# Weights converted with the sign set by ScalarE's parametric ReLU; retention with 64-row score matmuls, q scaled on GpSimd and x split from PSUM

## The chip, the cores and the metric

The kernel runs on one core of one Trainium2 chip. The metric is the device time of one execution in microseconds (us), median of several runs. Engines are named as in the profile: PE is TensorE (its matmuls; PEld its weight loads), DVE is VectorE, ACT is ScalarE, POOL is GpSimd, SP is SyncE, whose queue issues all DMAs here.

## The reference

Four batches of 576 tokens and 8 heads of 64 go through retention (attention with a decay and no softmax), and then through two MLPs of 512 x 2048. All weights arrive as float64.

```
scores = scale * (q @ k.T)
ret    = scores * D          # D[i, j] = gamma_h ** (i - j) for i >= j, else 0
x      = (ret @ v), heads side by side: 2304 tokens x 512
x1     = square(relu(x @ w_in)) @ w_out            # first MLP
h      = x1 @ w_in2
out    = (h * clip(h + 3, 0, 6) / 6) @ w_out2      # second MLP
```

## The kernel before, in words

**Numbers.** A product in about full float32 is made of three fp32r matmuls: weight and input are each split in a rounded part (index 0) and the rest (index 1), and the three larger products are added up in PSUM. So each of the 16 slices of d_ff (f) costs 12 matmuls into `h` (`h_part`, line 296) and 12 (second MLP, 384 tokens: 9) into the accumulators `acc` (`a_part`, lines 340 and 342). Retention's own matmuls are plain fp32; the trace shows each of these as two instructions.

**Weights.** Each slice has two halves (512 columns of w_in, 512 of w_out), and each half is converted from the 64 bits of its float64 numbers. `scale_w`: ACT multiplies the high word as if it were a float32 (line 109) and turns the low word into rounding bits (line 110). `narrow_w`, on DVE: shift the high word left (124), put the sign bit back from the high word (125), and add the low bits as an integer (127, on POOL for the second MLP's w_out halves, else on DVE). `split_w`: a rounded part by ACT (138) or DVE (136), and the rest by a subtraction on POOL (139). The 32 halves of the first MLP are converted during its first block of 512 tokens; the 32 of the second are spread over 27 steps, from the first MLP's last block into the second MLP's first block.

**Retention** goes by chunks of 128 tokens. `prep_chunk` scales v (POOL; chunk 0 on DVE). `scores` multiplies k by q for each of 8 heads: k is kept by the dims of two heads, one head at a time, with noughts in the other head's 64 rows, so that every matmul uses all 128 rows (204); DVE applies the mask from PSUM (210). `values` makes `o` (223, and 233 for the state of earlier chunks), scales it by the query's decay (246 on DVE, or 243 on ACT and 244 on POOL for chunks 0 to 2), and splits x: rounded part on ACT (249), rest on POOL (250). `states` carries the state on (262, 274 to 277).

**Order.** The schedule is manual: every engine takes its instructions in program order and waits by semaphores. First come chunks 0 to 3, then 160 steps of (MLP, block, f). A step issues `h_part` of the next step before `a_part` of its own, with weight conversions and a quarter of the next block's chunk (prep, scores, values, states, one in each of four steps) in between. In the first block the step's DVE work is: `narrow_w` of a w_out half, its rounded part, the split of `g`, and `narrow_w` of a w_in half. In the first block ACT makes all of `r` and of the rounded `g` (306, 308, 316); in the other blocks DVE squares (310) and rounds (318).

## Time and profile before

| | us |
|---|---|
| runs | 928.20, 926.77, 928.01 (median 928.01) |
| span of the profiled execution, first to last instruction | 924.4 |
| PE busy | 891.0 (96%) |
| DVE busy | 499.9 (54%) |
| ACT busy | 240.3 (26%) |
| POOL busy | 205.9 (22%) |

The profiled execution's time is shown as its span alone; the runs lie 2.4 to 3.8 us above it, which is what stands before the first and behind the last instruction. A busy PE is not a PE at its peak, since matmuls are pipelined and their ends are modelled: how fast PE goes is read from start to start. The averages hide three kinds of stage. DVE is busy nearly all the time in two of them, about 32 to 144 us and 480 to 595 us, and lightly used in the rest.

### The profile page before, as it was taken

Reading aid. Unit: us, or ns where it says so; the run is one execution under the profiler, and the core shown is the slowest. Engines: PE = TensorE matmul, PEld = TensorE weight load, DVE = VectorE, ACT = ScalarE, POOL = GpSimd, SP = SyncE. Lnnn points to the kernel's source line nnn. Section 1 sums busy time; section 2 is a strip of 40 time slices with the busy share of each in tenths; the row PEclk is TensorE's granted clock in tenths of the full one; section 3 lists DMA queues with packets and bytes.
Section 4 is the critical chain, followed back from the end, with each engine's and each line's share of the span. In section 5 each row is a group of like instructions: output and inputs, shape, how many; then the busy total and the mean of one; then the engine's idle time right before and its main releaser. Section 6 shows DMA issues by size and latency. Waiting matters only on the chain.

```text
span 924.4 us, 11741 instructions
## 1 busy us (share of the span) xinstructions
PE 891.0 (96%) x4716; PEld 760.1 (82%) x4716; DVE 499.9 (54%) x772; ACT 240.3 (26%) x411; POOL 205.9 (22%) x169
## 2 busy tenths in 40 slices
PE   7899999999999999999999997899999999999998
PEld 6677768999888899998877786788888888888997
DVE  5899995433433334433889899633343334333333
ACT  2666662111111111112444553211111111111111
POOL 5555551110101001120356356300100110010000
PEclk9899999999999999999999999999999999999999
DMA  8934511121201111105565300100020002000100
GB/s 287 364 100 155 206 46 46 46 69 47 80 23 46 46 46 46 46 1 166 202 215 169 126 0 12 59 11 1 12 80 1 12 0 72 1 9 0 46 1 35
DMA packets 26549, 67.73 MB, mean 73 GB/s; under 512 B 3200, under 2 KB 5376, under 8 KB 26496
## 3 DMA queue, kind: packets, MB, share of 16 engines
q1 hardware_dynamic: 26496, 67.00, 21.2%
q8 instruction: 37, 0.61, 0.3%
q14 instruction: 16, 0.13, 0.0%
HBM read 57.55 MB, written 9.44 MB: 72 GB/s over the span
## 4 chain that ended last, share of the span: by engine, by line
PE 72%; DVE 17%; DMA 5%; issue 3%; ACT 2%; POOL 1%; SPq 1%; DVEq 0%; ACTq 0%; POOLq 0%
PE h L296 33%; PE acc L342 18%; PE acc L340 15%; DVE wt L127 4%; DVE wt L125 4%; DVE wt L124 3%; DVE g L319 2%; PE sc L204 2%; DMA raw<-w_dram 2%; DVE g L318 2%; DMA kt<-qk_dram 1%; PE o L223 1%; PE o L233 1%; ACT r L306 1%; DVE r L313 1%
## 5 line engine op out<-in xcount | busy, mean ns | idle before, releaser
L296 PE MATMUL h<-x,w 128*128 128x512 f32 (+2 forms) x1932 | 425.9, 368 | 5.3 <-ACT w L138 3.0
L296 PEld LDWEIGHTS h<-x,w 128*128 128x128 f32 x1932 | 352.3, 188 | 57.7 <-POOL w L139 5.7
L340 PE MATMUL acc<-g,w 128*128 128x512 f32 (+1 forms) x960 | 217.2, 373 | 5.1 <-POOL w L139 1.8
L342 PE MATMUL acc<-w,g 128*128 128x512 f32 x864 | 212.8, 393 | 9.1 <-DVE g L318 8.2
L342 PEld LDWEIGHTS acc<-w,g 128*128 128x128 f32 x864 | 160.8, 188 | 46.1 <-DVE g L318 9.8
L340 PEld LDWEIGHTS acc<-g,w 128*128 128x128 f32 x960 | 172.0, 188 | 31.6 <-POOL w L139 3.9
L313 DVE SCALAR_TENSOR_TENSOR r<-r,h 128x512 f32<-128x512 f32 (+1 forms) x80 | 50.7, 633 | 202.9 <-ACT r L312 202.9
L310 DVE TENSOR_TENSOR r<-r 128x384 f32<-128x384 f32 (+1 forms) x64 | 42.3, 662 | 173.0 <-ACT r L306 172.9
L312 ACT ACTIVATE r<-h,con 128x512 f32<-128x512 f32 (+1 forms) x80 | 51.5, 644 | 283.0 <-PE h L296 274.4
L319 DVE TENSOR_TENSOR g<-r,g 128x512 fp32r<-128x512 f32 (+1 forms) x160 | 120.7, 754 | 6.3 <-ACT g L316 1.3
L139 POOL TENSOR_TENSOR w<-wt,w 128x512 fp32r<-128x512 f32 x64 | 96.4, 1510 | 82.3 <-ACT w L138 48.8
L306 ACT ACTIVATE r<-h 128x512 f32<-128x512 f32 (+1 forms) x80 | 44.1, 551 | 240.5 <-PE h L296 231.4
L318 DVE CAST g<-r 128x512 fp32r<-128x512 f32 (+1 forms) x144 | 71.6, 497 | 14.3
L385 POOL TENSOR_TENSOR x<-x1r,x 128x512 fp32r<-128x512 f32 (+1 forms) x20 | 25.4, 1271 | 240.1 <-DVE x L384 238.4
L250 POOL TENSOR_TENSOR x<-x,x 128x512 fp32r<-128x512 f32 (+1 forms) x19 | 23.6, 1245 | 208.7 <-ACT x L249 208.7
L125 DVE SCALAR_TENSOR_TENSOR wt<-raw,wt 128x512 int32<-128x512 int32 x64 | 58.3, 911 | 2.2
L138 ACT ACTIVATE w<-wt 128x512 fp32r<-128x512 f32 x48 | 30.3, 631 | 87.4 <-DVE wt L127 53.4
L127 DVE CUSTOM_DVE_ANT_0 wt<-raw,wt 128x1024 uint16<-128x1024 uint16 x48 | 46.9, 977 | 3.5
L204 PE MATMUL sc<-q,kt 128*128 128x128 f32 x288 | 38.0, 285 | 5.8 <-POOL kt L392 4.2
L204 PEld LDWEIGHTS sc<-q,kt 128*128 128x128 f32 x288 | 36.4, 199 | 7.4 <-POOL kt L392 4.2
L109 ACT ACTIVATE raw<-raw 128x512 f32<-128x512 f32 x64 | 42.5, 663 | 0.0
L110 ACT ACTIVATE raw<-raw 128x512 int32<-128x512 uint32 x64 | 42.4, 662 | 0.0
(33 smaller groups left out, 325.0 us busy)
## 6 DMA issues: line engine op xcount, KB each, us to landing
raw<-w_dram SPq DMA_DIRECT2D x64, 512.0 KB, 6.0
kv<-kv_dram SPq DMA_DIRECT2D x14, 512.0 KB, 3.2
q<-qk_dram SPq DMA_DIRECT2D x18, 256.0 KB, 2.9
kt<-qk_dram SPq DMA_DIRECT2D x36, 128.0 KB, 3.1
out_dram<-ev SPq DMA_DIRECT2D x18, 256.0 KB, 2.3
x<-ev SPq DMA_DIRECT2D x12, 256.0 KB, 2.1
x1r<-x SPq DMA_DIRECT2D x12, 256.0 KB, 3.5
kv<-kv_dram SPq DMA_DIRECT2D x8, 256.0 KB, 5.4
```

The lines of the kernel that those rows point to most:

```text
L125: nc.vector.scalar_tensor_tensor(ti, high, -(2**31), ti, ALU.bitwise_and, ALU.bitwise_or)
L127: eng.tensor_tensor(ti, ti, low, ALU.add)
L139: nc.gpsimd.tensor_tensor(w[:, 1, :], t, w[:, 0, :].bitcast(F32), ALU.subtract)
L204: nc.tensor.matmul(sc[e][:, p, :], kt[:, e, p, :], q[:, p, :], start=True, stop=True)
L296: nc.tensor.matmul(hp[:, ts], w[:, wi, c * P : (c + 1) * P], x[:, xi, c, ts], start=k == 0, stop=k == 3 * NC - 1,)
L306: nc.scalar.activation(r, hp[:, :nb], AF.Relu)
L312: nc.scalar.activation(r, hp[:, :nb], AF.Relu, bias=con3)
L313: nc.vector.scalar_tensor_tensor(r, r, 6.0, hp[:, :nb], ALU.min, ALU.mult)
L318: nc.vector.tensor_copy(g[:, 0, :nb], r)
L319: nc.vector.tensor_tensor(g[:, 1, :nb], r, g[:, 0, :nb].bitcast(F32), ALU.subtract)
L340: nc.tensor.matmul(acc[d][:, :nb], wt[:, sl], gt, start=first, stop=stop)
L342: nc.tensor.matmul(acc[d], gt[:, sl], wt, start=first, stop=stop)
```

## The change

Weights: ACT's scaling of the high word becomes a parametric ReLU with the slope -(2^32) for negative numbers. A negative number comes out positive, with an exponent that the shift by three turns into a set sign bit, so DVE's instruction for the sign goes. The integer addition is now on DVE for all halves. Retention: q is scaled by its decay ahead of the scores (POOL; chunk 0 on DVE), so `o` needs no factor and x is split directly from PSUM, rounded part on ACT and rest on DVE. k comes without noughts, in one DMA, and a head's scores use the 64 rows of that head alone, the two heads of a pair in turn. The table of q's factors is loaded earlier. First MLP: `r` times `h` from PSUM on DVE replaces the square, in the first block that on ACT.

```diff
-            nc.scalar.activation(high.bitcast(F32), high.bitcast(F32), AF.Copy, scale=2.0**-112)
+            high = high.bitcast(F32)
+            nc.scalar.activation(high, high, AF.Prelu, scale=2.0**-112, alpha=-(2.0**32))
...
-            nc.vector.scalar_tensor_tensor(ti, high, -(2**31), ti, ALU.bitwise_and, ALU.bitwise_or)
-            eng = nc.gpsimd if ph and i else nc.vector
-            eng.tensor_tensor(ti, ti, low, ALU.add)
+            nc.vector.tensor_tensor(ti, ti, low, ALU.add)
...
-        for e in range(2):
-            r = slice(64 * e, 64 * e + 64)
-            nc.sync.dma_start(kt[r, e], qk[c, r, 1, :].rearrange("p (n t) -> p n t", n=NPAIR))
+        if c == 0:
+            nc.sync.dma_start(con[:, QD0:], cst[:, QD0:])
+        nc.sync.dma_start(kt, qk[c, :, 1, :].rearrange("p (n t) -> p n t", n=NPAIR))
...
     def prep_chunk(c, eng):
+        q = ch[c][0]
+        eng.tensor_tensor(q, q, qd3, ALU.mult)
...
-                nc.tensor.matmul(
-                    sc[e][:, p, :], kt[:, e, p, :], q[:, p, :], start=True, stop=True
-                )
+                r = slice(64 * e, 64 * e + 64)
+                nc.tensor.matmul(sc[e][:, p, :], kt[r, p, :], q[r, p, :], start=True, stop=True)
...
-            t = tmpp.tile([P, np_, P], F32, tag="tmp", name=f"x_{c}_{i}")
             hi = xt[:, 0, ps, off : off + P]
-            if c < n0 and parts == 1:
-                nc.scalar.activation(t, o, AF.Copy)
-                nc.gpsimd.tensor_tensor(t, t, qd3[:, ps], ALU.mult)
-            else:
-                nc.vector.tensor_tensor(t, o, qd3[:, ps], ALU.mult)
+            nc.scalar.activation(hi, o, AF.Copy)
             if then is not None:
                 then()
-            nc.scalar.activation(hi, t, AF.Copy)
-            nc.gpsimd.tensor_tensor(xt[:, 1, ps, off : off + P], t, hi.bitcast(F32), ALU.subtract)
+            nc.vector.tensor_tensor(xt[:, 1, ps, off : off + P], o, hi.bitcast(F32), ALU.subtract)
...
             nc.scalar.activation(r, hp[:, :nb], AF.Relu)
-            if blk == 0:
-                nc.scalar.activation(r, r, AF.Square)
-            else:
-                nc.vector.tensor_tensor(r, r, r, ALU.mult)
+            nc.vector.tensor_tensor(r, r, hp[:, :nb], ALU.mult)
...
-    for t in kts:
-        for e in range(2):
-            nc.gpsimd.memset(t[64 * e : 64 * e + 64, 1 - e], 0.0)
```

How instructions move on the engines: first DVE in the first block of the first MLP, in the step that prepares w_out half 2 and, behind it, w_in half 4 (`wt` is a half's float32, `raw` its words, `g` the input of the second product, `p` the masked scores). Before:

```order
L124 TENSOR_SCALAR wt_2_1_480<-raw_2_1_152 128x512
L125 SCALAR_TENSOR_TENSOR wt_2_1_480<-raw_2_1_152,wt_2_1_480 128x512
L127 ISA wt_2_1_480<-raw_2_1_152,wt_2_1_480 128x1024
L136 CAST w_2_1_487<-wt_2_1_480 128x512
L319 TENSOR_TENSOR g_0_2_506<-r_0_2_503,g_0_2_506 128x512
L210 TENSOR_TENSOR p_4_523<-sc_4_513,con 128x512
L210 TENSOR_TENSOR p_4_525<-sc_4_514,con 128x512
L124 TENSOR_SCALAR wt_4_0_527<-raw_4_0_448 128x512
L125 SCALAR_TENSOR_TENSOR wt_4_0_527<-raw_4_0_448,wt_4_0_527 128x512
L127 ISA wt_4_0_527<-raw_4_0_448,wt_4_0_527 128x1024
```

and now:

```order
L126 TENSOR_SCALAR wt_2_1_448<-raw_2_1_136 128x512
L127 ISA wt_2_1_448<-raw_2_1_136,wt_2_1_448 128x1024
L136 CAST w_2_1_454<-wt_2_1_448 128x512
L298 TENSOR_TENSOR r_0_2_470<-r_0_2_470,h_0_2_457 128x512
L307 TENSOR_TENSOR g_0_2_473<-r_0_2_470,g_0_2_473 128x512
L207 TENSOR_TENSOR p_4_490<-sc_4_480,con 128x512
L207 TENSOR_TENSOR p_4_492<-sc_4_481,con 128x512
L126 TENSOR_SCALAR wt_4_0_494<-raw_4_0_416 128x512
L127 ISA wt_4_0_494<-raw_4_0_416,wt_4_0_494 128x1024
```

Two sign instructions are gone, and the multiplication of `r` stands between the cast and the split of `g`; the ACT instruction that rounds `g` stands, in its own queue, between these two.

Second, POOL in the first steps of the first block, where the weights' rests (`w`) and chunk 4's preparation (`kv`, `q`) share the queue. Before:

```order
L139 TENSOR_TENSOR w_2_0_419<-wt_2_0_415,w_2_0_419 128x512
L139 TENSOR_TENSOR w_1_1_426<-wt_1_1_422,w_1_1_426 128x512
L190 TENSOR_TENSOR kv_216<-kv_216,con 128x512
L139 TENSOR_TENSOR w_3_0_484<-wt_3_0_456,w_3_0_484 128x512
L139 TENSOR_TENSOR w_2_1_487<-wt_2_1_480,w_2_1_487 128x512
```

and now:

```order
L139 TENSOR_TENSOR w_2_0_388<-wt_2_0_385,w_2_0_388 128x512
L139 TENSOR_TENSOR w_1_1_394<-wt_1_1_391,w_1_1_394 128x512
L186 TENSOR_TENSOR q_199<-q_199,con 128x512
L188 TENSOR_TENSOR kv_200<-kv_200,con 128x512
L139 TENSOR_TENSOR w_3_0_451<-wt_3_0_425,w_3_0_451 128x512
L139 TENSOR_TENSOR w_2_1_454<-wt_2_1_448,w_2_1_454 128x512
```

The scaling of q comes behind the weights' rests and ahead of v's; a chunk's scores, one step later on PE, now need it.

## Rows read from the trace of the kernel before

**Rows 1.** The page's first line.

```profile
span 924.4 us, 11741 instructions
```

**Rows 2.** Three stretches of the windows view: the first block of the first MLP; its blocks 1 to 3; and the stage of the second MLP's weights. Columns: stretch and its length; busy us and instructions of PE, PEld, DVE, ACT, POOL; granted clock; DMA share; GB/s.

```profile
31.80:143.70 111.90, 105.96 (x554) 81.70 (x553) 106.03 (x141) 72.13 (x125) 58.88 (x43) 1.00 0.43 152
143.70:414.80 271.10, 271.10 (x1730) 247.52 (x1730) 108.03 (x202) 35.62 (x65) 34.60 (x37) 1.00 0.14 46
...
479.50:595.20 115.70, 100.93 (x458) 83.02 (x457) 104.85 (x133) 51.74 (x92) 60.82 (x43) 0.99 0.22 73
```

**Rows 3.** Timeline of PE in block 1 (384 tokens). Columns here and in the other timelines: start us, duration us with the drain of the last one, engine, line, operation, out<-in, shape, count, and in brackets the idle time before it with its releaser.

```profile
152.80 2.24 PE L296 MATMUL h<-x,w 128*128 128x384 f32 x12
154.88 1.95 PE L204 MATMUL sc<-q,kt 128*128 128x128 f32 x16
156.58 2.33 PE L340 MATMUL acc<-g,w 128*128 128x384 f32 x12
158.76 2.24 PE L296 MATMUL h<-x,w 128*128 128x384 f32 x12
160.93 1.09 PE L223 MATMUL o<-p,kv 128*64 128x128 f32 x16
161.96 1.16 PE L233 MATMUL o<-q,state 128*128 128x128 f32 x8
...
167.23 0.69 PE L262 MATMUL st<-kv 128*64 128x64 f32 x16
...
176.28 1.95 PE L204 MATMUL sc<-q,kt 128*128 128x128 f32 x16
```

**Rows 4.** Timeline of PE in the first block (512 tokens): the scores of chunks 5 and 6, four steps apart.

```profile
74.71 1.95 PE L204 MATMUL sc<-q,kt 128*128 128x128 f32 x16
...
104.17 1.95 PE L204 MATMUL sc<-q,kt 128*128 128x128 f32 x16
```

**Rows 5.** Timeline of DVE in the first block.

```profile
112.43 0.42 DVE L124 TENSOR_SCALAR wt<-raw 128x512 int32<-128x512 int32 x1
112.88 0.69 DVE L125 SCALAR_TENSOR_TENSOR wt<-raw,wt 128x512 int32<-128x512 int32 x1
113.61 0.69 DVE L127 CUSTOM_DVE_ANT_0 wt<-raw,wt 128x1024 uint16<-128x1024 uint16 x1
...
115.50 1.57 DVE L127 CUSTOM_DVE_ANT_0 wt<-raw,wt 128x1024 uint16<-128x1024 uint16 x1
...
118.05 0.68 DVE L246 TENSOR_TENSOR x<-o,con 128x512 f32<-128x512 f32 x1
```

**Rows 6.** Timeline of POOL in the first block.

```profile
115.04 1.48 POOL L139 TENSOR_TENSOR w<-wt,w 128x512 fp32r<-128x512 f32 x1 [2.70 <-ACT w L138]
```

**Rows 7.** Timeline of PE in the stage of the second MLP's weights: the start of four groups of h.

```profile
479.54 0.84 PE L296 MATMUL h<-x,w 128*128 128x512 f32 x3
...
521.71 2.27 PE L296 MATMUL h<-x,w 128*128 128x384 f32 x12
...
525.90 2.27 PE L296 MATMUL h<-x,w 128*128 128x384 f32 x12
...
595.20 2.88 PE L296 MATMUL h<-x,w 128*128 128x512 f32 x12
```

**Rows 8.** Timeline of DVE in the same stage.

```profile
522.43 0.36 DVE L318 CAST g<-r 128x384 fp32r<-128x384 f32 x1
...
525.35 0.55 DVE L313 SCALAR_TENSOR_TENSOR r<-r,h 128x384 f32<-128x384 f32 x1
526.00 1.04 DVE L318 CAST g<-r 128x384 fp32r<-128x384 f32 x1
527.07 0.56 DVE L319 TENSOR_TENSOR g<-r,g 128x384 fp32r<-128x384 f32 x1
...
528.00 1.67 DVE L125 SCALAR_TENSOR_TENSOR wt<-raw,wt 128x512 int32<-128x512 int32 x1
...
560.55 0.42 DVE L384 CAST x<-x1r 128x512 fp32r<-128x512 f32 x1
```

**Rows 9.** Timeline of POOL in the same stage.

```profile
525.51 1.31 POOL L127 TENSOR_TENSOR wt<-wt,raw 128x512 int32<-128x512 int32 x1 [1.56 <-DVE wt L125]
```

**Rows 10.** Timeline of DVE in the first 32 us.

```profile
19.57 1.41 DVE L125 SCALAR_TENSOR_TENSOR wt<-raw,wt 128x512 int32<-128x512 int32 x1
21.13 1.54 DVE L127 CUSTOM_DVE_ANT_0 wt<-raw,wt 128x1024 uint16<-128x1024 uint16 x1
...
24.35 1.31 DVE L277 TENSOR_TENSOR state<-state,con 64x256 f32<-64x256 f32 x1
```

**Rows 11.** Timeline of PE there: chunk 3's values.

```profile
26.35 1.12 PE L223 MATMUL o<-p,kv 128*64 128x128 f32 x8 [3.31 <-DVE state L276]
```

**Rows 12.** The groups by line. Columns: line, engine, operation, out<-in, shapes, count | busy us, mean ns | idle us before and its releasers.

```profile
L109 ACT ACTIVATE raw<-raw 128x512 f32<-128x512 f32 x64 | 42.5, 663 | 0.0
...
L316 ACT ACTIVATE g<-r 128x512 fp32r<-128x512 f32 x16 | 10.1, 632 | 0.5
...
L243 ACT ACT_TABLE_LOAD x1 | 1.3, 1283 | 0.7 <-PEq L521 0.7
```

**Rows 13.** The weight loads of the scores (128 columns) and of the values (64 columns), from the view of one line. Columns: duration ns min/median/max, first and last start, forms.

```profile
L204 PEld LDWEIGHTS sc<-q,kt x288: 186/192/338, 4.2 to 406.2; 128*128 128x128 f32 x144
...
L223 PEld LDWEIGHTS o<-p,kv x288: 132/137/232, 12.2 to 411.4; 128*64 128x64 f32 x144
```

More of the change, by code (lines that the diff above doesn't have):

```diff
@@ L147, in retention_moe_kernel @@
     state = [apool.tile([P, NPAIR, P], F32, tag=f"s{i}", name=f"state{i}") for i in range(2)]
-    kts = [apool.tile([P, 2, NPAIR, P], F32, tag=f"kt{i}", name=f"kt{i}") for i in range(2)]
-    kts += [wpool.tile([P, 2, NPAIR, P], F32, tag=f"w{NF - 1}_{i}", name=f"kt{i + 2}") for i in range(2)]
     n0 = BLOCKS[0][0][0] // P
@@ L162, in load_chunk @@
             kv_t = wpool.tile([P, 2, DM], F32, tag=f"w{NF - 3}_{c % 2}", name=f"kv_{c}")
-            q, kt = t[:, 0], kts[c]
         else:
-            q = rawp.tile([P, NPAIR, P], F32, tag="q", name=f"q_{c}")
+            t = rawp.tile([P, 2, NPAIR, P], F32, tag="q", name=f"q_{c}")
             kv_t = rawp.tile([P, 2, DM], F32, tag="kv", name=f"kv_{c}")
-            kt = kts[c % 2]
+        q, kt = t[:, 0], t[:, 1]
         nc.sync.dma_start(q, qk[c, :, 0, :].rearrange("p (n t) -> p n t", n=NPAIR))
-        for e in range(2):
-            r = slice(64 * e, 64 * e + 64)
-            nc.sync.dma_start(kt[r, e], qk[c, r, 1, :].rearrange("p (n t) -> p n t", n=NPAIR))
+        if c == 0:
+            nc.sync.dma_start(con[:, QD0:], cst[:, QD0:])
+        nc.sync.dma_start(kt, qk[c, :, 1, :].rearrange("p (n t) -> p n t", n=NPAIR))
         if c == 0:
@@ L397, in retention_moe_kernel @@
     load_chunk(1)
-    nc.sync.dma_start(con[:, QD0:], cst[:, QD0:])
     load_chunk(2)
```

## The prediction

> **What bounds the kernel now.** I read the windows by stage first. In blocks 1 to 3 PE is busy for all of the 271.1 us and DVE for 108: PE bounds, and only PE work taken away counts. In the first block and in the stage of the second MLP's weights DVE is busy for 106.0 of 111.9 us and 104.9 of 115.7, while PE has gaps [rows 2]. After 595 us nothing changes. So there are four places: the start, the two stages of DVE, and retention on PE in between.
>
> The timelines then give rates. On PE a group of 12 matmuls of 384 columns starts the next one 2.08 us later where 2.24 is printed, so 0.16 is drain [rows 3]; 12 of 512 columns, printed as 2.88, take 2.72 [rows 7]. A step of 512 tokens is thus 5.44 us on PE, and a step of the second MLP's block of 384 takes 525.90 - 521.71 = 4.19 [rows 7].
>
> On DVE the same instruction has two durations. The addition takes 0.69 us, and 1.57 where it begins inside a subtraction of POOL (115.04 to 116.52) [rows 5, 6]; the sign instruction takes 0.69 or 1.67 [rows 5, 8], the cast 0.36 or 1.04 [rows 8]. An instruction on SBUF data that meets one of POOL is held, by 0.9 to 1.0 us. Those that read PSUM (0.68 and 0.55) show no such stretch in these rows [rows 5, 8]. DVE's load is therefore its own work plus POOL's instructions as far as they meet it.
>
> **The change part by part.**
>
> *Start.* Chunk 3's values wait 3.31 us for DVE [rows 11]. Ahead of them on DVE stand a sign instruction (1.41, goes), a held addition (1.54) and a held state update (1.31, by its shape no longer than 0.69) [rows 10]. POOL's scaling and subtraction of x, which hold them, go. I count 1.41 for the sign, 0.85 and 0.6 for the holds, a second 0.6 for the other half's update, less 0.69 for a subtraction of x that DVE gains: 2.8, say 3. Upper bound the whole wait, 3.3. Lower bound -1: chunk 0's scores now need the table and a DVE multiplication of about 0.69 first.
>
> *First block.* Chunks 5 and 6 lie 104.17 - 74.71 = 29.46 us apart, four steps [rows 4]. In these DVE loses 8 sign instructions, 8 x 0.69 = 5.5, and gains 4 multiplications from PSUM, 4 x 0.69 = 2.8 (priced as the 0.68 of such an operand). It also gains a wait: the split of `g` stands right behind the multiplication and needs ACT's rounding in between, 0.63 [rows 12] and two hand-overs, some 0.73 a step or 2.9 in four, and 0.6 once where x's subtraction waits for ACT. Queued behind these waits are the next half's shift and addition. But POOL's subtraction for the w_out half starts behind the cast, so it now runs under the multiplication and the wait (1.4 us together), and its hold goes: 4 x 0.88 = 3.5. The other holds stay; on POOL q's scaling replaces x's subtraction. Sum: 29.46 - 5.5 + 2.8 + 2.9 + 0.6 - 3.5 = 26.7. PE could do it in 4 x 5.44 + 4.64 for retention (block 1's chunks are 176.28 - 154.88 = 21.40 apart, less four steps of 4.19 [rows 3, 7]) less 0.6 = 25.8, so PE is close behind as the next bound. The stage's 111.9 us are 3.8 such cycles [rows 2]; I count 3.6, since the first h at its start is not paced by DVE. Gain 3.6 x 2.76 = 9.9. Bounds: 13 if DVE falls to PE's 25.8, and 0 if the holds stay and the waits come on top (30.2, rounded to no gain).
>
> *Scores.* 16 instructions take 156.58 - 154.88 = 1.70 us, 106 ns each. The nearest row in which neighbours use different halves of the array is that of the values: 161.96 - 160.93 = 1.03 [rows 3]. There the halves are of columns, here of rows. I take 1.03 and add 0.09 for the change of shape: 2.17 us from h to o against 2.08 from h to scores [rows 3]. 1.70 - 1.12 = 0.58 a chunk, in the 11 chunks of blocks 1 to 3: 6.4. Upper bound two full halves, 0.85 and so 0.76 a chunk, 8.4; lower bound below nothing, see the first rival. Block 0's three chunks are inside its term.
>
> *Second MLP's weights.* From 479.54 to 595.20 PE does 10 groups of 512 columns and 16 steps of 4.19: 27.2 + 67.0 = 94.2 of 115.7 us, so 21.4 are lost [rows 7]. 32 halves in 27 steps are 1.19 a step. DVE's step before: 0.55 + 0.36 + 0.56 for `r` and `g` [rows 8], 1.19 x (0.42 + 0.69) for shift and sign, 0.59 x 0.69 for the additions that it has, 3.2 in all; and 1.78 POOL instructions (1.19 subtractions, 0.59 additions of 1.31 [rows 9]) at a hold of 0.98, 1.7: 4.9 against PE's 4.19. Now shift and addition, 1.19 x 1.11, and 1.19 holds: 1.47 + 1.32 + 1.17 = 3.96, under 4.19. What stays late are the four steps that also cast a piece of x1 (0.42 [rows 8]) and meet its POOL subtraction (0.98): 5.4 against 4.19, 1.2 x 4 = 5. Gain 21.4 - 5 = 16.4. Upper bound 21.4; lower bound what DVE loses by itself, 32 x 0.69 - 16 x 0.69 = 11.
>
> *At nothing.* The parametric ReLU instead of a copy: 0.66 [rows 12], and even twice that would be 32 x 0.66 = 21 us more in a block where ACT idles for 40 of 112 [rows 2]; that idle time is its cover. q's 14 later scalings on POOL, at about 1.3 each: POOL idles for more than 230 of the 271 us of blocks 1 to 3 [rows 2], and a whole step lies between preparation and scores. Fewer DMA issues and the earlier table: in the term of the start. The squares of the other blocks: DVE idles there.
>
> **Sum.** 3 + 9.9 + 6.4 + 16.4 = 35.7 off the span of 924.4 [rows 1]: 888.7. The runs' median stands 3.6 above that span, so 892.3; I say 892.
>
> **The rivals.**
>
> 1. *Weight loads pace the scores* (15%). A load of 128 columns is printed 55 ns longer than one of 64 (192 against 137) [rows 13], 0.86 ns a column, so 110 for 128 columns; if loads went one by one, 16 would take 1.76 us however few rows they have, and with 0.09 the scores would be 0.15 slower than 1.70: -1.7 instead of +6.4, 900. Against it: the state's 16 instructions, each with a load of 64 columns, are printed as 0.69 with their drain [rows 3], under the 16 x 55 = 0.88 of loads one by one. That was between halves of columns; for rows nothing shows it. The Trainium skill has this rival as a rule ("TensorE: Matmul & The Clock Gate", section LDWEIGHTS): a load takes its columns over 1.2 GHz, whatever the rows, an estimated 1.71 us for 16 of 128 columns. Applied one by one it would give the state's 16 loads an estimated 0.85, and the trace does not agree.
>
> 2. *The first block stays bound by DVE* (15%). The new order DVE, ACT, DVE inside each step, with in-order queues on both, costs what the sign instruction gave; the bound above, no gain there: 902. For it: DVE has hardly any idle time there to put the wait in.
>
> 3. *Both stages fall to PE's pace* (8%): 13 and 21.4 instead of 9.9 and 16.4: 884; with the upper bounds of the others, 882.
>
> 4. *Slower: ACT changes tables* (3%). If the parametric ReLU is not held together with copy and ReLU, each of its 64 uses needs two table loads of 1.28 us [rows 12]. In the first block ACT, busy for 72.1 of 111.9 [rows 2], less 16 squares of 0.63 (line 308 is of the kind of line 316), would get 32 x 2.56 = 82 more: 144 against the 102 forecast, 42 more; in the later stage 51.7 + 82 = 134 against 99, 35 more: 892 + 77 = 969. It decides from about three uses in four: ACT's idle time, 40 and 47, covers the first, and 164 x 0.75 - 87 = 36 is the sum above. Against it: the changed program's ACT queue, like the one before, begins with one table load and has no other. The Trainium skill ("ScalarE: Activation LUTs", section Table sets: the hidden batching unit) says that cheap functions such as relu and copy are in every set and only a switch of sets costs; its section on the evaluator also says that the parametric ReLU's slope select is not reachable from a kernel, which would make wrong weights and not another time.
>
> That q on POOL stalls PE at the scores is no case of its own: it would cost chunk 4 once, where the queue is full with the first weights.
>
> **How the numbers follow.** The forecast has 59%, the rivals 15, 15, 8 and 3. The forecast's own range is 885 to 900: its terms' bounds seldom fall to one side together. Rivals 1 and 2 lie at 900 and 902, both together, or with the lower bound of the late stage, at 908; rival 3 at 882. I give 882 to 907, which leaves out rival 4 and the ends of combinations. A measurement of this kernel tells apart about 0.2%, 1.9 us. All cases but the fourth are faster by far more: faster 0.95, same 0.02 for a sum of mishaps, slower 0.03.
>
> **What would show it.** Scores of 16 instructions in about 1.1 us in block 1; chunks 5 and 6 about 26.7 us apart, with a wait of some 0.7 ahead of the split of `g`; in the stage of the second MLP's weights one held DVE instruction a step where there are two, and PE's 115.7 us down to about 99; the rest after it as long as before. I am wrong if scores stay at 1.7, if the chunks stay 29 apart, if DVE's instructions in the late stage are held as often as now, or if ACT shows table loads.

## The result, and the profile after

The changed kernel takes 892.73 us (median of 4 runs, 892.26 to 893.54) against 927.53 for the kernel before in the same session: a ratio of 0.963, with an interval of 0.9617 to 0.9645. The forecast was 892. The profiled execution's span fell from 924.4 to 891.1 us.

I cut both traces at the same five places, read from PE's timeline, and use the table for every run below. *Start*: up to the first `h`. *First block*: to the first `h` of 384 columns. *Blocks 1 to 3*: to the first `h` of 512 columns behind the last state product. *Late*: to the second group of `h` of 512 columns behind the second MLP's first block (595.20 in [rows 7]); it is the stretch of 115.7 us in [rows 2] and the 64.7 us ahead of it, which the change left as they were. *Rest*: to the end.

| us | start | first block | blocks 1 to 3 | late | rest | span |
|---|---|---|---|---|---|---|
| before | 31.82 | 111.92 | 271.06 | 180.40 | 329.20 | 924.4 |
| after | 28.42 | 104.10 | 265.55 | 163.63 | 329.40 | 891.1 |
| gain | 3.40 | 7.82 | 5.51 | 16.77 | -0.20 | 33.3 |
| forecast | 3 | 9.9 | 6.4 | 16.4 | 0 | 35.7 |

The windows of the changed kernel, with the columns of [rows 2]: first block, blocks 1 to 3, the stage of the second MLP's weights, and a piece of the first block.

```profile
28.42:132.52 104.10, 100.60 (x557) 81.02 (x554) 89.21 (x127) 60.93 (x108) 53.15 (x41) 0.98 0.44 162
132.52:398.07 265.55, 265.55 (x1730) 237.87 (x1728) 109.72 (x202) 35.34 (x66) 35.39 (x37) 1.00 0.14 47
462.86:561.70 98.84, 96.24 (x457) 82.60 (x456) 87.62 (x122) 52.72 (x92) 40.96 (x31) 1.00 0.26 85
43.60:48.00 4.40, 4.40 (x15) 3.49 (x14) 3.57 (x5) 2.08 (x5) 2.75 (x3) 0.63 0.00 0
```

Against [rows 2], DVE's load fell from 106.0 to 89.2 us in the first block and from 104.9 to 87.6 in the late stage, and it is idle for longer in both: 104.10 - 89.21 = 14.9 and 98.84 - 87.62 = 11.2 us (in the first block 10.5 of it ahead of the splits of `g`, where DVE waits for ACT). In blocks 1 to 3 PE is busy all the time as before; only its own work became less.

PE's timeline in block 1, to be held against [rows 3]:

```profile
141.57 2.25 PE L287 MATMUL h<-x,w 128*128 128x384 f32 x12
143.74 1.16 PE L203 MATMUL sc<-q 64*128 64x128 f32 x16
144.84 2.35 PE L328 MATMUL acc<-g,w 128*128 128x384 f32 x12
```

From start to start the scores take 1.10 us where they took 1.70; the `h` ahead of them takes 2.17 where it took 2.08, which is the 0.09 for the change of shape.

PE's timeline in the first block, chunks 4, 5 and 6, beside [rows 4]:

```profile
42.48 1.20 PE L203 MATMUL sc<-q 64*128 64x128 f32 x16 [2.03 <-POOL q L186]
43.61 4.54 PE L328 MATMUL acc<-g,w 128*128 128x512 f32 x12
47.99 1.32 PE L287 MATMUL h<-x,w 128*128 128x512 f32 x5
...
70.13 1.16 PE L203 MATMUL sc<-q 64*128 64x128 f32 x16
...
96.90 1.23 PE L203 MATMUL sc<-q 64*128 64x128 f32 x16 [0.24 <-POOL q L186]
```

Chunks 5 and 6 are 26.77 us apart on PE; forecast 26.7, before 29.46. (DVE's own cycle is longer, as shown below.) At chunk 4 PE waits 2.03 us for POOL, and the next 12 matmuls take 47.99 - 43.61 = 4.38 us where such a group takes 2.72 [rows 7]. The last window above shows why: the granted clock is 0.63 there, a mean between the levels of 1.2 and 2.4 GHz.

DVE's timeline in the first block, beside [rows 5], and POOL's beside [rows 6]:

```profile
113.60 1.41 DVE L136 CAST w<-wt 128x512 fp32r<-128x512 f32 x1
114.93 0.68 DVE L298 TENSOR_TENSOR r<-r,h 128x512 f32<-128x512 f32 x1
116.30 0.69 DVE L307 TENSOR_TENSOR g<-r,g 128x512 fp32r<-128x512 f32 x1 [0.70 <-ACT g L304]
```

```profile
113.33 1.39 POOL L139 TENSOR_TENSOR w<-wt,w 128x512 fp32r<-128x512 f32 x1 [3.20 <-ACT w L138]
115.09 1.30 POOL L139 TENSOR_TENSOR w<-wt,w 128x512 fp32r<-128x512 f32 x1 [0.37 <-DVE w L136]
```

The wait of 0.70 ahead of the split of `g` is there. POOL's second subtraction (115.09 to 116.39) lies under the multiplication from PSUM, which shows its 0.68, and the wait, as I had put it. But the first one, which waits for ACT's rounding, now falls on the cast and stretches it to 1.41.

DVE in the late stage, beside [rows 8]:

```profile
515.53 0.36 DVE L306 CAST g<-r 128x384 fp32r<-128x384 f32 x1
515.93 1.56 DVE L307 TENSOR_TENSOR g<-r,g 128x384 fp32r<-128x384 f32 x1
```

One instruction is held in this step (the split of `g`, 1.56 where it takes 0.56), where the step of [rows 8] had two. PE takes its groups in this stretch without a gap.

The groups by line, beside [rows 12]:

```profile
L110 ACT ACTIVATE raw<-raw 128x512 f32<-128x512 f32 x64 | 42.5, 664 | 0.0
...
L238 ACT ACT_TABLE_LOAD x1 | 1.3, 1283 | 0.7 <-PEq L505 0.7
```

The parametric ReLU costs what the copy did, and there is one table load.

### The profile page after: what moved, and what is told of

Its sections match the earlier page's. It is cut to its first block, busy times and chain, and to the rows that moved or that the text cites. A ratio compares the mean times of both kernels' runs of the same rounds, so it can differ in the third digit from the quotient of the medians.

```text
span 891.1 us, 11679 instructions
## 1 busy us (share of the span) xinstructions
PE 871.0 (98%) x4716; PEld 745.5 (84%) x4716; DVE 458.5 (51%) x744; ACT 227.5 (26%) x392; POOL 164.3 (18%) x140
## 4 chain that ended last, share of the span: by engine, by line
PE 87%; DMA 6%; DVE 3%; issue 2%; POOL 1%; SPq 0%; ACT 0%; DVEq 0%; POOLq 0%; ACTq 0%
PE h L287 40%; PE acc L328 21%; PE acc L330 21%; DMA raw<-w_dram 3%; PE sc L203 2%; PE o L220 2%; PE o L230 2%; DMA q<-qk_dram 1%; DVE g L306 1%; PE st L253 1%; DVE wt L127 1%; DVE wt L126 1%; DMA kv<-kv_dram 1%; DMA x1r<-x 0%; POOL w L139 0%
## 5 line engine op out<-in xcount | busy, mean ns | idle before, releaser
L330 PEld LDWEIGHTS acc<-w,g 128*128 128x128 f32 x864 | 161.2, 188 | 35.7 <-DVE g L306 2.5
L298 DVE TENSOR_TENSOR r<-r,h 128x512 f32<-128x512 f32 (+1 forms) x80 | 50.6, 632 | 164.4 <-ACT r L297 164.3
L307 DVE TENSOR_TENSOR g<-r,g 128x512 fp32r<-128x512 f32 (+1 forms) x160 | 123.7, 773 | 16.2 <-ACT g L304 11.2
L139 POOL TENSOR_TENSOR w<-wt,w 128x512 fp32r<-128x512 f32 x64 | 87.9, 1377 | 155.8 <-ACT w L138 86.3
L268 POOL TENSOR_TENSOR state<-state,con 64x256 f32<-64x256 f32 x18 | 11.1, 619 | 207.0 <-DVE state L267 206.4
L203 PE MATMUL sc<-q 64*128 64x128 f32 x288 | 23.5, 307 | 10.3 <-DMA q<-qk_dram 6.0
L203 PEld LDWEIGHTS sc<-q 64*128 64x128 f32 x288 | 19.8, 208 | 15.2 <-DVE q L186 6.0
L126 DVE TENSOR_SCALAR wt<-raw 128x512 int32<-128x512 int32 x64 | 31.5, 491 | 0.5 <-issue 0.3
```

The source lines that it names most:

```text
L139: nc.gpsimd.tensor_tensor(w[:, 1, :], t, w[:, 0, :].bitcast(F32), ALU.subtract)
L203: nc.tensor.matmul(sc[e][:, p, :], kt[r, p, :], q[r, p, :], start=True, stop=True)
L298: nc.vector.tensor_tensor(r, r, hp[:, :nb], ALU.mult)
L307: nc.vector.tensor_tensor(g[:, 1, :nb], r, g[:, 0, :nb].bitcast(F32), ALU.subtract)
L330: nc.tensor.matmul(acc[d], gt[:, sl], wt, start=first, stop=stop)
```

## The experiments

All times are medians; ratios are against the kernel before in the same session. Stages are those of the table above.

| run | edited | us | ratio (interval) | start | first block | blocks 1 to 3 | late |
|---|---|---|---|---|---|---|---|
| e1_rows64 | before | 921.09 | 0.9933 (0.9913 to 0.9953) | 32.97 | 111.48 | 265.55 | 179.08 |
| e2_sign | before | 897.30 | 0.9674 (0.9650 to 0.9698) | 32.44 | 99.12 | 271.06 | 164.47 |
| e3_add_dve | before | 926.24 | 0.9984 (0.9969 to 0.9999) | 34.17 | 111.04 | 271.05 | 179.33 |
| e4_heads_apart | after | 899.78 | 0.9706 (0.9686 to 0.9727) | 28.79 | 105.61 | 271.77 | 163.51 |
| e5_square_act | after | 890.07 | 0.9602 (0.9585 to 0.9620) | 27.46 | 100.23 | 265.55 | 165.62 |
| e6_prep4_early | after | 892.14 | 0.9615 (0.9601 to 0.9629) | 28.02 | 103.57 | 265.55 | 164.08 |
| e7_pool_twice | after | 916.92 | 0.9886 (0.9867 to 0.9906) | 27.88 | 104.04 | 265.55 | 187.02 |
| e8_pool_memset | after | 894.44 | 0.9642 (0.9623 to 0.9661) | 27.42 | 103.74 | 265.55 | 165.29 |
| e9_both | after | 887.80 | 0.9574 (0.9557 to 0.9592) | 28.15 | 98.83 | 265.55 | 164.05 |
| e10_x1_act | e9 | 888.09 | 0.9577 (0.9560 to 0.9593) | 28.47 | 98.88 | 265.55 | 164.49 |
| e11_qx | before | 926.88 | 0.9994 (0.9985 to 1.0004) | 34.34 | 111.16 | 271.05 | 180.98 |
| e12_tmp4 | e10 | 885.91 | 0.9552 (0.9537 to 0.9566) | 27.46 | 98.88 | 265.55 | 162.76 |

### The scores: rows alone, and rows without alternation

e1 gives the kernel before the scores of 64 rows, and nothing else.

```diff
+                r = slice(64 * e, 64 * e + 64)
                 nc.tensor.matmul(
-                    sc[e][:, p, :], kt[:, e, p, :], q[:, p, :], start=True, stop=True
+                    sc[e][:, p, :], kt[r, e, p, :], q[r, p, :], start=True, stop=True
                 )
```

> The kernel before with the 64-row score matmuls alone (the noughts stay in the tile but are not read; q is not scaled, k's DMAs are as before). Theory (neighbouring matmuls in different row halves run at the same time): 16 instructions in about 1.10 us instead of 1.70, a switch of shape of 0.09 ahead of them, so 0.51 a chunk in the 11 chunks of blocks 1 to 3, 5.6 us off; nothing in the first block, whose pace DVE sets, and under 1 us at the start: 921 to 922 where before has 927.5. Rival (weight loads pace the scores): 1.7 to 1.8 us for the 16, 927 to 929.

Blocks 1 to 3 took 265.55 us, the same as in the whole change: this stage's gain of 5.51 is the scores' and nothing else's, 0.50 for each of 11 chunks. e4 takes the changed kernel and orders its 16 score instructions so that one head's come next to each other: the same instructions, but neighbours use the same 64 rows.

```diff
-        for p in range(NPAIR):
-            for e in range(2):
+        for e in range(2):
+            for p in range(NPAIR):
```

> The changed kernel with the scores' loops swapped: all four matmuls of the upper 64 rows, then all four of the lower, so that neighbours use the same rows. Theory (the gain is two matmuls at the same time): back to about 1.7 us for the 16, +0.6 in each of 11 chunks of blocks 1 to 3 and some at the start, 899 to 901 where the changed kernel has 892.7. Rival (a matmul over 64 rows is cheaper by itself, or its load is): 1.1 us as now, 892.7.

PE's timeline in block 1 of e4:

```profile
145.63 1.71 PE L203 MATMUL sc<-q 64*128 64x128 f32 x16
147.27 2.03 PE L328 MATMUL acc<-g,w 128*128 128x384 f32 x10
```

147.27 - 145.63 = 1.64 us, 103 ns each on the mean, and blocks 1 to 3 take 271.77: more than before the change by 0.7, since the change of shape is still paid. The single instructions of the three traces say more. Neighbours in the same rows start 112 ns apart before the change, in the changed kernel and in e4 alike, so a matmul of 64 rows is by itself no cheaper than one of 128. In the changed kernel the instructions of two heads, in different halves of rows, start 6 ns apart (143.743 and 143.750) and run side by side. What keeps the 16 at 1.10 us instead of half of 1.70 are two longer distances, 0.21 behind the first pair and 0.20 ahead of the next `acc`, at the changes of shape. e4 is under 1.70 because its second half of rows begins (146.19) while the first still has three instructions to start. The Trainium skill ("TensorE: Matmul & The Clock Gate", section The mechanism) has it that a weight load overlaps with matmuls in flight only where the group of rows differs; a sentence above that, it also lets a load into the background weight buffer be pulled ahead. Between the changed kernel and e4 the trace agrees with the first. 12 matmuls of 128 rows, each with its own load, take 2.72 us [rows 7], 227 ns each for 512 columns, so loads into the same rows are hidden too; whether by that buffer, no run here shows. Were weight loads taken one by one whatever the rows (the first rival), the order of heads would not matter and 1.10 us would not be possible.

### The sign, and the rest of the first block

e2 gives the kernel before the parametric ReLU and takes out the sign instruction; additions stay where they were.

```diff
+            high = high.bitcast(F32)
-            nc.scalar.activation(high.bitcast(F32), high.bitcast(F32), AF.Copy, scale=2.0**-112)
+            nc.scalar.activation(high, high, AF.Prelu, scale=2.0**-112, alpha=-(2.0**32))
...
-            nc.vector.scalar_tensor_tensor(ti, high, -(2**31), ti, ALU.bitwise_and, ALU.bitwise_or)
```

> The kernel before with the sign set by the parametric ReLU alone; additions stay where they were, retention as before. Theory (DVE's own work plus POOL's holds pace both stages): first block four steps in 27 instead of 29.5, -8; late stage DVE's step 4.9 - 0.82 = 4.1, just under PE's 4.19, so about 6 of 21.4 us stay lost, -15; start -1.5: 903 where before has 927.5. Rival (POOL's additions and subtractions of x are the larger part, and the sign instruction only gives its slots to longer holds): -8 to -12 in all, 916 to 920.

The first block falls to 99.12, by 12.8 where the whole change gains 7.8, and the late stage to 164.47, by 15.9 of the 16.8. Both are more than the 8 and 15 expected, and the median of 897.30 lies below the 903 of the theory: chunks 4, 5 and 6 come 26.57 us apart, where the prediction counts 4 x 5.44 + 4.64 = 26.4 for PE with scores of 128 rows, so PE sets the pace of this block. So the sign is the change in both stages, and something else in it costs the first block some 5 us. e5 puts the square of the first block back on ACT in the changed kernel:

```diff
-            nc.vector.tensor_tensor(r, r, hp[:, :nb], ALU.mult)
+            if blk == 0:
+                nc.scalar.activation(r, r, AF.Square)
+            else:
+                nc.vector.tensor_tensor(r, r, hp[:, :nb], ALU.mult)
```

> The changed kernel with r in the first block squared on ACT again, as before; all else as changed. It takes DVE's multiplication (0.69) and the wait of 0.70 ahead of the split of g out of each step. Theory (DVE, ACT, DVE inside a step keeps the first block above PE's pace): four steps in about 25.9, PE's own pace, instead of 26.8: -3, 889 to 890 where the changed kernel has 892.7. Rival (the wait only takes time that POOL's holds would take anyway, or PE is the bound already): 892 to 893.

The first block takes 100.23, 3.9 less, and its chunks come 26.1 us apart: against the 25.8 that I had counted for PE alone, that is nearly PE's pace. The median is 2.7 under the changed kernel's 892.73, from another session; the spans, 888.2 against 891.1, say the same. e6 instead goes for the wait at chunk 4: `prep_chunk(4)` is issued on POOL directly behind the first `h`, ahead of the weights' subtractions that stood before it in POOL's queue.

```diff
     h_part(0, 0, 0)
+    prep_chunk(n0, nc.gpsimd)
...
-                        prep_chunk(c, nc.gpsimd)
+                        if c > n0:
+                            prep_chunk(c, nc.gpsimd)
```

> The changed kernel with chunk 4's preparation on POOL moved ahead of the rests of the weight halves 2_0 and 1_1. Theory (the 2.03 us that PE waits for q at chunk 4's scores are lost, and the 12 matmuls behind them take 4.4 instead of 2.8 us at a granted clock of 0.63): -2 to -3.5, 889 to 890.5 where the changed kernel has 892.7. Rival (what PE loses there it would lose a few steps later on DVE): 892 to 893.

Expected were 889 to 890.5; the rival came. The wait is gone, and with it the slow clock; chunk 4's scores come 12.58 us behind the first `h` instead of 14.06, and chunk 5's 1.35 earlier. But the block is only 0.5 shorter, and the median (892.14) can't be told from 892.73. What PE gained was given back, because DVE sets the pace there. e8 below, whose first block is the changed kernel's, says the same: PE waits 2.01 us at chunk 4, the clock stays full behind it, and the block takes 103.74. e9 does e5 and e6 together (both diffs above):

> The changed kernel with both edits: r of the first block squared on ACT, and chunk 4 prepared ahead of the first weights' rests. With the square on ACT the first block ran at PE's pace (26.1 us a chunk) and PE still came to chunk 4's scores 13.96 us after its first h, where 11.3 were needed with the sign alone. Theory (time that PE loses comes back only where DVE sets the pace): now the 2 to 2.7 us are kept, 887.5 to 888.5 where the square alone gave 890.1. Rival (they are given back again): 890.

Where PE sets the pace the same edit is worth more: 98.83 against 100.23 in the block, and 887.80 against 890.07. In e5, by the way, the wait at chunk 4 is as long, but the clock does not fall behind it. PE's timeline and the window behind the scores:

```profile
41.42 1.16 PE L203 MATMUL sc<-q 64*128 64x128 f32 x16 [2.04 <-POOL q L186]
```

```profile
42.50:46.90 4.40, 4.40 (x21) 3.66 (x20) 4.20 (x6) 4.10 (x8) 3.31 (x3) 1.00 0.00 2
```

### What holds DVE in the late stage

e3 moves the addition of the second MLP's w_out halves from POOL to DVE in the kernel before, and nothing else: 16 more instructions of 0.69 on the engine that bounds the stage.

```diff
-            eng = nc.gpsimd if ph and i else nc.vector
+            eng = nc.vector
```

> The kernel before with all integer additions on DVE, nothing else changed. Only the late stage can move. Theory (a POOL instruction that reads SBUF holds DVE by 0.98): DVE gains 16 additions of 0.69, 11.0 us, and loses up to 16 holds of 0.98, 15.7: -2 to -5, 922.5 to 925.5 where before has 927.5. Rival (DVE is bound by its own instructions): +8 to +11, 936 to 938.

It costs nothing, and gains less than the 2 to 5 expected: 926.24 against 927.5, with an interval that just leaves out 1, and the late stage is 1.1 shorter. DVE's timeline of e3 shows the trade in one step: the shift, the sign and the addition take their unheld times, the split of `g` alone is held.

```profile
544.69 1.56 DVE L319 TENSOR_TENSOR g<-r,g 128x384 fp32r<-128x384 f32 x1
546.18 0.41 DVE L124 TENSOR_SCALAR wt<-raw 128x512 int32<-128x512 int32 x1
546.62 0.69 DVE L125 SCALAR_TENSOR_TENSOR wt<-raw,wt 128x512 int32<-128x512 int32 x1
547.35 0.69 DVE L127 CUSTOM_DVE_ANT_0 wt<-raw,wt 128x1024 uint16<-128x1024 uint16 x1
```

e7 doubles the suspected cost in the changed kernel: POOL makes each subtraction of the second MLP's weights twice.

```diff
             nc.gpsimd.tensor_tensor(w[:, 1, :], t, w[:, 0, :].bitcast(F32), ALU.subtract)
+            if ph:
+                nc.gpsimd.tensor_tensor(w[:, 1, :], t, w[:, 0, :].bitcast(F32), ALU.subtract)
```

> The changed kernel with each POOL subtraction of a second-MLP weight half issued twice (32 more instructions of 1.3 us that read SBUF, in queue order; POOL has the time). Theory (each holds DVE by about 0.98): DVE's step in the late stage 3.96 + 1.17 = 5.1 against PE's 4.19, so +14 in 16 steps and some in the steps of 512 ahead: +13 to +18, 906 to 911. Rival (POOL's load does not reach DVE): 892 to 894.

e8 gives POOL as much work in the same place that reads nothing: two memsets of a tile that nobody uses.

```diff
+    idle = cpool.tile([P, DM], F32, tag="idle", name="idle")
...
+            if ph:
+                for _ in range(2):
+                    nc.gpsimd.memset(idle, 0.0)
```

> The changed kernel with two POOL memsets of 128x512 into a tile that nobody reads behind each POOL subtraction of a second-MLP weight half: as much more POOL time, but it only writes. Theory (only instructions that read SBUF hold DVE): 892 to 894. Rival (any POOL instruction holds DVE): +8 to +15, 901 to 908.

The late stage grows by 23.4 us with the 32 reading instructions (more than the 13 to 18 expected), and by 1.7 with the 64 writing ones, which take 37.6 us of POOL against 47.7 for the 32. DVE's and POOL's timelines of e7, and e8's memsets among the groups by line:

```profile
527.50 1.55 DVE L309 TENSOR_TENSOR g<-r,g 128x384 fp32r<-128x384 f32 x1
528.98 1.51 DVE L126 TENSOR_SCALAR wt<-raw 128x512 int32<-128x512 int32 x1
```

```profile
527.34 1.30 POOL L139 TENSOR_TENSOR w<-wt,w 128x512 fp32r<-128x512 f32 x1 [1.35 <-ACT w L138]
528.72 1.49 POOL L141 TENSOR_TENSOR w<-wt,w 128x512 fp32r<-128x512 f32 x1
```

```profile
L142 POOL MEMSET idle<- 128x512 f32 x64 | 37.6, 588 | 1.8
```

Each POOL subtraction has its own held instruction on DVE (the split of `g`, then the shift, by 1.0 and 1.1). Over the stage that is 0.73 for each added one, less than a hold, since DVE's step was shorter than PE's without it (519.27 - 515.53 = 3.74 us from one rounding of `g` to the next, against 4.19). The memsets cost DVE next to nothing. So it is reading SBUF on POOL that holds DVE, not a busy POOL or its queue. The Trainium skill says so too ("SBUF — State Buffer", section Who interferes with whom): a VectorE instruction with two SBUF inputs is held by a GpSimd instruction that reads SBUF and not by one that only writes, and one with at most one SBUF input is held by none, but for copies, casts and operations with a scalar where they run in a mode that uses two ports. The trace agrees: the split of `g`, with two SBUF inputs, is held by 1.0 us, the shift, an operation with a scalar, by 1.1, which fits the exception, and a multiplication with one input from PSUM passes under a subtraction at 0.68.

### What is left of the late stage

Before, 21.4 us were lost there, so PE's own time is 180.40 - 21.4 = 159.0, and the changed kernel still loses 4.6. PE's timeline shows where:

```profile
496.77 2.34 PE L330 MATMUL acc<-w,g 128*128 128x512 f32 x9 [0.78 <-DVE g L306]
...
539.50 2.52 PE L330 MATMUL acc<-w,g 128*128 128x512 f32 x9 [0.61 <-DVE g L306]
541.86 2.27 PE L287 MATMUL h<-x,w 128*128 128x384 f32 x12
...
546.43 2.27 PE L287 MATMUL h<-x,w 128*128 128x384 f32 x12
...
551.98 0.96 PE L287 MATMUL h<-x,w 128*128 128x384 f32 x4 [0.82 <-ACT w L138]
553.34 1.68 PE L287 MATMUL h<-x,w 128*128 128x384 f32 x8 [0.40 <-POOL w L139]
...
556.94 2.88 PE L287 MATMUL h<-x,w 128*128 128x512 f32 x12
```

In the steps with a piece of x1 PE follows DVE at 4.56 us a step (546.43 - 541.86 = 4.57) where 4.19 is its own. The largest piece comes at their end: PE's last group of 384 columns waits for the two parts of a weight half, whose rounding on ACT in turn waited for DVE, and the last two steps take 551.98 - 546.43 = 5.55 and 556.94 - 551.98 = 4.96, together 2.1 over PE's own. e10 takes e9 and moves the rounding of x1 from DVE to ACT:

```diff
-        nc.vector.tensor_copy(x[:, 0, d, :], t[:, :nb])
+        if blk < 2:
+            nc.scalar.activation(x[:, 0, d, :], t[:, :nb], AF.Copy)
+        else:
+            nc.vector.tensor_copy(x[:, 0, d, :], t[:, :nb])
```

> As the kernel with both edits, and the rounded part of x1 for the second MLP's first two blocks made by ACT instead of DVE. Theory (what stays lost in the late stage, some 5 us, is the four steps in which DVE also casts x1): 0.42 off DVE in each of 4 steps whose need is about 5.4 against 4.19, -1.5 to -2 against the kernel with both edits. Rival (the holds by x1's own POOL subtraction are what counts): no difference over 0.5.

No gain, as the rival said: 888.09 against 887.80, and the steps are as long as they were. DVE's timeline of e10:

```profile
539.16 1.56 DVE L310 TENSOR_TENSOR g<-r,g 128x384 fp32r<-128x384 f32 x1
...
541.09 1.67 DVE L127 CUSTOM_DVE_ANT_0 wt<-raw,wt 128x1024 uint16<-128x1024 uint16 x1
...
543.72 1.56 DVE L310 TENSOR_TENSOR g<-r,g 128x384 fp32r<-128x384 f32 x1
```

543.72 - 539.16 = 4.56 again. DVE lost the cast, but POOL's subtraction of x1 now meets the addition (1.67) instead of the short rounding of `g`, and takes back as much. e12 then adds a fourth temporary buffer, for the wait at 496.77, which stands at the change from the first MLP to the second, where a transfer still reads one of the three:

```diff
-    tmpp = ctx.enter_context(tc.tile_pool(name="tmpp", bufs=3))
+    tmpp = ctx.enter_context(tc.tile_pool(name="tmpp", bufs=4))
```

> As the kernel with both edits and x1's rounded part on ACT, with four buffers instead of three for r and the evicted accumulators. Theory (one of the losses left, about 1 us where the first MLP ends, is a buffer that waits for a DMA of x1): -1 against the same kernel with three. Rival (the wait moves to the accumulators): no difference.

The late stage falls by 1.7, where 1 was expected; the wait at 496.77 is gone, and most of the rest comes from the last two steps. At 885.91 this is the best version of those that ran: 0.9552 of the kernel before, and 0.992 of the changed kernel (885.91 / 892.73, from two sessions).

### The start, and q and x

e11 gives the kernel before the early table, q scaled ahead of the scores and x split from PSUM; the scores keep 128 rows, and k its noughts and its two DMAs.

```diff
+        if c == 0:
+            nc.sync.dma_start(con[:, QD0:], cst[:, QD0:])
...
+        q = ch[c][0]
+        eng.tensor_tensor(q, q, qd3, ALU.mult)
...
-            t = tmpp.tile([P, np_, P], F32, tag="tmp", name=f"x_{c}_{i}")
...
+            nc.scalar.activation(hi, o, AF.Copy)
...
-            nc.scalar.activation(hi, t, AF.Copy)
-            nc.gpsimd.tensor_tensor(xt[:, 1, ps, off : off + P], t, hi.bitcast(F32), ALU.subtract)
+            nc.vector.tensor_tensor(xt[:, 1, ps, off : off + P], o, hi.bitcast(F32), ALU.subtract)
```

> The kernel before with retention's q and x alone: table loaded early, q scaled ahead of the scores, x split from PSUM on ACT and DVE; scores over 128 rows with noughts, k in two DMAs, weights and r as before. Theory (from chunk 3's scores to the first h the sign gave 1.9 of 4.3 us, POOL's absence from that stretch the rest): that distance 13.6 becomes 11 to 11.5, so -2 to -2.5; first block 0 to -1 (DVE still sets its pace, PE's wait for q at chunk 4 lies in its shadow); blocks 1 to 3 and the late stage as before: 924.5 to 925.5 where before has 927.5. Rival (q's two more POOL instructions a chunk hold DVE in the first block): first block +2 to +4, 927 to 929.

No difference that can be measured, where 2 to 2.5 less were expected. The start must be read in two pieces, since chunk 3's scores come at other times in every execution. From these scores to the first `h` it is 31.82 - 18.20 = 13.6 us before, 13.1 and 13.0 in e1 and e3, 11.7 with the sign alone (e2), 11.9 with q and x alone (e11), and 28.42 - 19.14 = 9.3 in the changed kernel. Sign and q with x thus save about 1.7 to 1.9 each; the whole change saves 4.3, so they add up, with some 0.7 for the rest. A part of this is the clock. Two windows from chunk 3's values to the first `h`, before and after, with the columns of [rows 2]:

```profile
26.35:31.82 5.47, 5.47 (x41) 4.24 (x41) 4.92 (x7) 1.47 (x4) 2.37 (x3) 0.50 1.04 337
```

```profile
24.31:28.42 4.11, 3.14 (x41) 2.42 (x41) 2.44 (x6) 2.23 (x6) 0.00 (x0) 1.00 1.03 399
```

PE has the same instructions there. Before, behind the wait of 3.31 us [rows 11], the granted clock is 0.50, the lower of its two levels, and PE is busy for 5.47 us; in the changed kernel, behind waits of 0.43 and 0.97, the clock is full and 3.14 are enough. The mean granted clock of this piece is 0.62 to 0.76 in e1, e2, e3 and e11, and 1.00 in all nine traces of the changed kernel and its variants. So 1.4 of the 4.3 us lie here, and they are what the full clock saves (2.3) less the 0.97 that PE still waits.

The other piece of the start is the time until chunk 3's scores. In e11 they came at 22.46, 4.3 us later than in the trace of before, which took the gain back. Most of that is scatter: e1, e2 and e3 have 19.8 to 21.1. Against e3, which does not touch the start (21.13), e11 loses 1.3, all of it ahead of chunk 1's scores, at 11.70 against 10.33:

```profile
11.70 3.78 PE L208 MATMUL sc<-q,kt 128*128 128x128 f32 x16 [2.39 <-POOL q L192]
```

They wait for q's scaling on POOL. One trace of each can't tell how much of the 1.3 is scatter, too. In the first block DVE's cycle of four steps is as long as before (29.4 us), because a hold only moves: from one split of `g` to the next, the step with chunk 5's values takes 6.75 us where it took 7.76 (x's subtraction is gone from POOL), and the step that prepares chunk 5 takes 8.36 where it took 7.44 (q's scaling has come). What k's single DMA is worth at the start was not tried alone.

## Why the prediction was right, point by point

- **The sum.** 33.3 us off the span against 35.7, and 1.6 us rather than 3.6 between span and median, which is why the total came out at 0.1%: two misses of about 2 us that cancel, so the nearness is luck. The second has a plain cause. I took the 2.4 to 3.8 us between span and runs for time ahead of the first and behind the last instruction; but wherever the record has a run's time and its own span, they differ by 1.7 to 1.9. The execution whose span is 924.4 was simply some 1.8 us faster than the median of its kernel. Between the medians the change gained 927.53 - 892.73 = 34.8, so the terms together are about 1 too large, not 2.4.
- **Blocks 1 to 3** (5.5 for 6.4). The mechanism holds, and e1 and e4 show it: halves of rows overlap as halves of columns do. The size was off because I took the 1.03 of the values with 0.09 on top, and the 16 scores alone are 1.10: 0.51 a chunk, not 0.58. 11 x 0.51 is 5.6.
- **Late stage** (16.8 for 16.4). Removing the sign is 15.9 of it (e2). Additions on DVE for all halves are worth about 1, since each takes a POOL instruction and its hold away (e3). That POOL's subtractions hold DVE once each is shown by e7 and e8. I left 5 to the steps with x1, and 4.6 are left, but mostly elsewhere: about 1 is the wait at the change of MLP, which I had not seen and e12 removed; about 1.4 lie in the steps with x1 themselves (539.50 and 541.86 in PE's rows), and 2.1 in the last two steps of 384 columns. A step with x1 costs 4.56, not 5.4: DVE prepares one half in it, not the mean of 1.19, and one of the holds falls on the rounding of `g`, which it lengthens by 0.67 and not by 0.98.
- **First block** (7.8 for 9.9). The 26.77 us between chunks 5 and 6 look like the 26.7 of the forecast, but that is luck: traces of kernels with the same first block have 26.72 (e7) and 27.96 (e8) there, since PE comes to the scores more or less far behind DVE. DVE sets the pace, and its own cycle, from the split of `g` of one step to that of the fourth step on, was not reached. DVE's timeline, eight steps apart, before and after:

```profile
44.74 0.68 DVE L319 TENSOR_TENSOR g<-r,g 128x512 fp32r<-128x512 f32 x1
...
103.07 0.68 DVE L319 TENSOR_TENSOR g<-r,g 128x512 fp32r<-128x512 f32 x1
```

```profile
40.60 0.69 DVE L307 TENSOR_TENSOR g<-r,g 128x512 fp32r<-128x512 f32 x1 [0.70 <-ACT g L304]
...
95.64 1.75 DVE L307 TENSOR_TENSOR g<-r,g 128x512 fp32r<-128x512 f32 x1 [0.70 <-ACT g L304]
```

  Four steps took (103.07 - 44.74) / 2 = 29.17 us and take (95.64 - 40.60) / 2 = 27.52: a gain of 1.65, where 2.76 was forecast. DVE's groups by line between the scores of chunks 5 and 6, before and after, show the parts:

```profile
L127 DVE CUSTOM_DVE_ANT_0 wt<-raw,wt 128x1024 uint16<-128x1024 uint16 x8 | 9.3, 1166 | 0.7
L125 DVE SCALAR_TENSOR_TENSOR wt<-raw,wt 128x512 int32<-128x512 int32 x8 | 7.6, 948 | 0.3
L124 DVE TENSOR_SCALAR wt<-raw 128x512 int32<-128x512 int32 x9 | 6.7, 740 | 0.0
...
L136 DVE CAST w<-wt 128x512 fp32r<-128x512 f32 x4 | 1.7, 427 | 0.1
```

```profile
L127 DVE CUSTOM_DVE_ANT_0 wt<-raw,wt 128x1024 uint16<-128x1024 uint16 x8 | 5.8, 730 | 0.7
L136 DVE CAST w<-wt 128x512 fp32r<-128x512 f32 x4 | 5.8, 1441 | 0.1
L126 DVE TENSOR_SCALAR wt<-raw 128x512 int32<-128x512 int32 x8 | 4.3, 532 | 0.0
L307 DVE TENSOR_TENSOR g<-r,g 128x512 fp32r<-128x512 f32 x4 | 3.8, 958 | 2.8 <-ACT g L304 2.8
L298 DVE TENSOR_TENSOR r<-r,h 128x512 f32<-128x512 f32 x4 | 2.7, 678 | 0.0
```

  The multiplication (2.7) and the wait ahead of the split (2.8) are as forecast. "The other holds stay" is not: the additions lost theirs (3.5 less), the sign instruction took its own along (7.6, not 5.5), the cast gained one in each step (4.1), and the split of `g` one of q's scaling (the 1.75 at 95.64). With the edges of the windows taken away, in the cycle that ends at that split (67.77 to 95.64, before 73.64 to 103.07), the sums are: sign -7.6, additions -3.5, shifts -0.9, multiplication +2.7, cast +4.1, split +1.1, idle time +2.5; that is -1.6.
- **The step of the prediction that was wrong** is thus the balance of holds in the first block's cycle: one hold goes in each step (3.5), and "The other holds stay". By the times that the same instructions take unheld (0.42, 0.43 and 0.69), DVE's holds went from 7.66 to 6.33 us in that cycle, by 1.3 only, because the subtraction that waits for ACT now meets the cast. The idle time was 1 less than I put it. That PE stands for 2.03 us at chunk 4, which I had priced at nothing, and then loses some 1.7 us at the lower clock, matters little beside that: without the wait the block is 0.5 shorter (e6), without the fall of the clock 0.4 (e8).
- **Start** (3.4 for 3). The sign's part and that of q and x are about 1.9 and 1.7 (e2, e11) where I had 1.41 and 0.85 + 0.6 + 0.6 - 0.69 = 1.36; a part of the saving is the clock, which fell in the start of before and not in the changed one, and which the prediction does not have. The total hangs on the execution: e3, with the start of before, has 34.17 where that trace has 31.82, and e5 to e10 have 27.4 to 28.5. So the nearness of 3.4 to the forecast proves little.
- **The rivals.** The first (weight loads one by one) is refuted by e4. The second did not occur, since the block gained 7.8, but its mechanism is there: DVE still sets the block's pace (27.5 us in four steps, 26.1 in e5), and the multiplication on DVE with its order DVE, ACT, DVE costs 3.9 (e5). The third is what e2 nearly reaches in the first block (99.12, a gain of 12.8 for its 13); the changed kernel does not. The fourth did not occur: there is one table load, and the slope does set the sign, for which the changed kernel has no other instruction.

## What to carry to other kernels

Count an engine's load with what holds it: here an instruction that reads SBUF, taken from GpSimd, saves VectorE a hold of 0.7 to 1.1 us, so moving work onto the engine that bounds can be free, while moving a rounding off it can gain nothing when the hold merely finds another instruction. Put a conversion's extra work into an instruction that an idle engine makes anyway (here the sign into ACT's scaling), and keep orders like DVE, ACT, DVE out of a stage that one of them bounds. A wait taken from an engine that doesn't set the pace is given back, so remove the pace first and then the wait.

## What the runs showed of the hardware

- Matmuls with 64 rows run side by side if neighbours use different halves of the rows: 16 fp32 instructions of 64 x 128 on 128 columns take 1.10 us in turn and 1.64 in two runs of eight, against 1.70 with 128 rows. In the same rows they start 112 ns apart with 64 rows as with 128.
- A POOL instruction that reads SBUF lengthens a DVE instruction on SBUF that it meets by 0.7 to 1.1 us; a POOL memset of the same tile hardly at all (32 reads +23.4 us, 64 memsets +1.7).
- Nearly the same stop of PE (2.01 to 2.04 us, at the same place) was followed by a lower granted clock in three traces (0.50 at its lowest, in the changed kernel, e4 and e7) and by none below full in two (e5, e8).
- Chunk 3's scores, near the start, came between 18.2 and 22.5 us in traces of the kernel before and its variants, which load the same bytes.
